# A second loop of pairs behind one branch, early reads for the first loop, and 86 unread products in the attention

## Chip, cores and metric

One NeuronCore of a Trainium2 chip runs the whole kernel. The metric is the device time of one execution in microseconds (us); three timed executions of the kernel before are known, and one more was taken with the hardware profiler. The engines are TensorE (PE; PEld is its weight load), VectorE (DVE), ScalarE (ACT), GpSimd (POOL) and SyncE (SP), which issues most DMAs. A q behind an engine's name means its sequencer.

## The reference

A Nyström attention with 32 landmarks over 8 batches, 8 heads, 576 tokens and 64 dimensions is followed by two mixture-of-experts layers on 4608 tokens with 8 experts each, top 1. Which expert gets how many tokens is known only at run time.

```python
A = sm(q, k_lm); Bm = sm(q_lm, k_lm); C = sm(q_lm, k)
Z = Bm.transpose(0, 1, 3, 2) / (norm(Bm, 1) * norm(Bm, inf) + 1e-06)
for _ in range(6):
    Z = 2 * Z - Z @ Bm @ Z
x = (A @ Z @ C @ v)            # rows of 512
for e in range(E):             # layer 0
    h = np.maximum(x[mask] @ w1[e], 0.0)
    out[mask] = gate_w[mask, None] * eom[mask, e, None] * (h @ w2[e])
for e in range(E):             # layer 1, routed by x @ w_gate + modality_bias
    h = np.maximum(x[mask] @ w1[e], 0.0)
    out[mask] = gate_w[mask, None] * (h @ w2[e])
```

## The kernel before

**Attention.** The work of the 8 batches is cut into small steps. A string `ORDER` lists them, a word each (batch and step), and the generators of the steps are advanced in that order, so it sets the order of the instructions on every engine. Its last words are `0st` and `0tab`: `st` is `static`, the first four tiles of layer 0's MoE (128 tokens each, the busiest expert's first 512 rows), and `tab` is `tile_table`, which works out on DVE, from the experts' counts, a table with one partition per further tile: the row to load, the piece of weights to load, and the parity (`PAR`). `numi` holds the number of tiles and of experts at work. Rows of tokens are scattered by POOL into a DRAM region `reg` with one stretch per expert (`scatter`, L684 clears a few words, L685 is the indirect DMA); `k.scat` lists these DMAs.

**A tile.** `steps` runs `h = relu(x @ w1)` (L1271) and `y = h @ w2` (L1322). Values are split into a high and a low fp16 part (`whi`, `wlo`; `hh` from ACT at L1279, `hl` from DVE at L1282), with three products for each. `xl` holds the 1024 x 128 transposed tokens, loaded by a DMA transpose from SP (L1066); `PLANS` says behind which product each other part runs (`after1`: the next tile's `xl`, behind the last product that reads this one). `L1152` is the product of the routing of the tile before, `L1143` the copy into the rows of the next layer, `L1203` their scatter.

**Loops.** Behind the static tiles eight products (L1692) are issued whose result nobody reads. Then every engine reads two registers (`reg_load`, L836, from `pari` and `numi`), SP loads the first rows (`x_load` in `tiles`), and `tiles(0, ...)` loops over the remaining tiles of layer 0, 34 with these inputs. Three static tiles of layer 1 follow, and then `tiles(1, ...)`, whose turns take two 128-row tiles at once (`pair`, products of 256 columns, L1388 and L1415, tokens in `xab`) or a single one (`alone`). With these inputs all its 17 turns are pairs. Each turn picks one of four bodies by two branches:

```python
with tc.If(odd > 0) as c:
    with tc.If(par < 2) as d:
        alone_(1)
    with d.Else():
        pair_(1)
```

TensorE, and every other engine, runs its instructions in the order in which they are written, and register reads and branches stand in that order too.

Of the kernel before, what the change touches and what calls it, by code (L numbers as in the profile page):

```python
# [26 lines left out]
E = 8  # L27
# [31 lines left out]
1mb0 1w0 2sc0 2sa0 1w1 1ws 3t2 2sc0 2sc1 1mb1 3t0 0x0 1ws 1ws 0x0 1mb0 3t3 2sc1 1ws 2sa0 2sa0 2ct0 2sc1 1mb1 1ws 2n
1ws 2n 1ws 2sa0 1ws 0x0 0f1 2ct0 2n 0f1 2ct1 2sa1 2ct1 0f1 1wg1 2sa1 3ld2 1wk0 2bt0 0f1 2ct1 2ct1 2sa1 2cv1 2n 1wk1  # L60
1wg1 2sa1 0f1 1wg1 2n 3t3 1wg0 2ct0 0x0 2bt1 0f1 3t2 2cv1 1wg1 2ma0 1wg0 2ma1 0f1 3t5 2n 3ld3 1wg0 1wg0 0x0 2ct0
0f1 2ma0 4ld2 1x3 3t0 2n 0f1 1x3 1x3 3t4 2bt0 2n 4ld0 0f1 1x1 2bt1 1x1 1x3 1x1 3t5 0f1 1x3 3t6 2cv0 3t6 2ma0 2ma1
1x1 2n 3sc0 2cv0 1x1 0f1 2ma1 4t5 3t4 2bt0 0f1 2bt1 0f1 1x4 1x4 0f1 1x4 2ch0.0 3sc0 0f1 3sc0 3t7 2ch0.1 2ch0.1
2ch1.1 2ch0.0 4t1 2ch1.0 1x4 2mb1 3sc0 2ch1.1 2ch1.0 0f1 1x2 1x4 2mb0 2mb1 2mb0 2mb0 2ch2.1 1x2 2ch2.0 1x0 4t0
2ch2.1 2ch2.0 1x2 2mb1 2ch3.1 2ch3.0 2ch3.1 2ch3.0 1x2 3t7 2ch4.1 1x2 2ch4.1 2ch4.0 3ct0 4t5 1x0 2ch4.0 4t0 0f2
2mb0 3ct0 2ch5.1 2mb0 2mb1 1x0 2ch5.0 2ch5.0 3sc1 0s1 2w0 2w0 1f1 3ct0 2ch5.1 2mb1 0s2 2w1 3ct0 4t4 2w1 3sc1 1f1
3sc1 2ws 3sa1 3sc1 1f1 0s3 2ws 3sa1 3sa0 3sa0 3n 3n 3sa0 3ct1 3sa0 3n 4t4 3ct1 2ws 2ws 3n 3ld4 3ct1 0s0 2ws 3sa1 3n
2ws 3ct1 0s4 2ws 3cv0 2ws 2wk0 2wg1 1f1 3sa1 1x0 3cv0 1f1 2wg0 3ma1 3bt0 4ld3 3n 2wg1 2wg1 2wg0 3n 1f1 4ld1 3n 2wk1
2wg1 1x0 1f1 3bt1 3cv1 2wg0 3ma1 4t1 4t2 4t3 3n 2wg0 3ma1 3cv1 3bt0 3bt1 2x1 3ma0 3bt1 4t6 2x2 4t7 2x1 2x1 3bt0
3ch0.1 3mb1 3ch0.1 3ch0.0 2x1 4t2 2x2 3ch1.1 1f1 3ch0.0 2x2 1f1 2x2 3ch1.1 5ld0 2x1 3ch2.1 1f1 4t3 3ch1.0 1f1 2x2  # L70
1f1 5ld2 1f1 1f1 3mb1 2x3 4sc0 1f1 3mb1 3ch1.0 2x3 3ma0 5t4 3ch2.0 3ch2.1 4t6 2x3 4t7 1f1 2x3 3ch2.0 3ch3.1 2x3
4sc0 3ch3.1 3ch3.0 3ch3.0 4sc0 0c 4sc1 3ch4.1 4sc1 1f1 3ch4.0 4sc1 3ma0 4sc0 4ct0 3ch4.0 3ch4.1 3ch5.0 4ld4 3ch5.1
4sc1 3mb0 3ch5.0 2x0 3ch5.1 4n 3mb0 2x4 4n 4ct0 5t0 1f2 3w1 3mb1 1s2 3w0 4sa1 5t4 3mb0 3mb1 4n 1s4 3mb0 3w1 3w0 3ws
2x4 4n 1s1 4sa1 3mb0 4ct1 4bt0 3ws 4sa1 4n 2x4 4ct1 3ws 4sa1 2x0 1s3 5ld3 2x4 3ws 4sa0 2x0 4n 4ct1 4ma1 2f1 4sa0 4n
2x0 4sa0 4ma1 3ws 4ct1 2x4 4n 3ws 4n 5ld1 4cv1 4bt0 1s0 3ws 4sa0 3ws 4bt1 6ld3 2x0 4bt0 4cv1 4ct0 3wg1 3wk1 4bt1
2f1 3wg1 4ct0 2f1 4cv0 3wg1 4ma1 3wg0 4bt1 4cv0 4ma0 2f1 3wg1 4ch0.1 3wg0 5t0 4ch0.1 4ch0.0 2f1 3wg0 4ch0.0 3wk0
2f1 4ch1.1 4mb1 3wg0 4ma0 4ch1.0 2f1 4ch1.1 4ma0 5t2 3x3 4ch1.0 3x3 3x3 3x1 3x1 5t3 4mb1 4ch2.1 4ch2.0 3x3 4mb0 2f1
6ld2 2f1 6t7 4ch2.1 4ch2.0 3x1 3x3 4ch3.0 4mb0 5t2 5t6 3x1 4ch3.1 5t1 3x0 2f1 5t3 4mb1 4ch3.0 4ch4.0 2f1 3x1 4ch3.1
2f1 3x0 2f1 5t6 3x0 4ch4.0 6t7 3x2 5ld4 4ch4.1 5t5 4ch4.1 3x0 4mb1 3x0 5t7 4mb0 2f1 5t1 4ch5.0 2f1 4ch5.1 4ch5.1
4ch5.0 5sa0 3x4 3x2 3x2 3x4 2f1 4w1 4w0 4mb0 5t5 3x4 4mb1 3x2 5t7 4mb0 5sa1 5sa0 3x2 2f1 6t5 5sa1 3x4 3x4 4w1 5sc1  # L80
3f1 4w0 2f2 5sc0 4ws 5sc1 2s0 4ws 5sa1 2s3 3f1 5sc1 6t6 5sc0 5sc0 5sa0 5sa1 4ws 3f1 5sa0 5sc1 5sc0 3f1 4ws 2s1 2s4
3f1 5ct1 5n 4ws 7ld2 5n 3f1 5ma0 5ct1 5ct1 3f1 5ct1 4ws 5ct0 5ct0 5n 5ct0 5ct0 5cv1 3f1 3f1 4ws 6ld0 5cv1 3f1 4ws
4wg0 3f1 3f1 5bt0 4wg0 2s2 5n 7t4 5cv0 3f1 3f1 6t6 4wk1 5n 6t5 4wg1 4wk0 4wg0 5cv0 5n 5bt1 4wg1 7ld3 5n 5ma0 4wg0
5n 4wg1 5bt0 4wg1 5bt1 5n 4x4 4x2 6t4 5bt0 5bt1 5ch0.0 5ma1 5ma0 7t5 3f1 4x4 5ch0.1 4x4 4x2 5ch0.0 4x4 0late 5ch0.1
5ch1.1 6t4 6ld1 5ch1.0 4x4 6sc1 7t4 3f1 5ch1.1 5ch2.1 5mb0 0late 6t1 5ch1.0 5ma1 6sc1 4x2 4x2 5ch2.0 3f1 5ma1 6t2
6sc1 5ch2.1 4x2 4x3 5ch2.0 5mb1 5ch3.1 7t5 6sc1 5ch3.0 0late 5ch3.1 4x3 4x1 5ch3.0 6t2 5mb1 3f2 5ch4.1 6t1 4x3
5ch4.0 0late 4x1 5mb0 5ch4.0 3s4 5ch4.1 7t6 4x3 6t3 4x1 5mb1 6ct1 5ch5.0 3s2 6t3 5ch5.0 6t0 5ch5.1 7t7 4x1 4x3 6ct1
5ch5.1 0late 5w0 5mb0 6t0 5w0 5w1 7t7 5w1 5ws 6sc0 4x1 7t6 4x0 5ws 5ws 6ld4 0late 6sc0 6sc0 5mb1 3s3 6sa1 5ws 5mb1
3s1 6sc0 6ct1 5ws 6sa1 6n 6sa1 5ws 6n 5mb0 6ct1 7ld1 4x0 5mb0 6n 6ct0 6sa0 5ws 6sa1 6cv1 6n 6ct0 5ws 6bt1 3s0 7ld0
6sa0 4x0 5wg1 6n 6bt0 6sa0 4f1 0late 5wg0 4f1 5wk1 6cv1 5wg1 5wk0 7t2 5wg1 6n 6sa0 4x0 5wg0 5wg0 5wg1 4f1 6n 4f1  # L90
4f1 5wg0 6bt1 6bt0 4x0 0late 6ct0 6n 4f1 6ct0 5x1 4f1 6cv0 5x1 6n 0late 6bt1 5x1 6ch0.1 5x4 7t0 5x1 6cv0 6bt0 6ma1
5x1 7t1 5x4 5x4 6ch0.0 6ma0 4f1 7sc1 4f1 7t3 7ld4 5x4 6ma1 6ch0.1 4f1 7t3 4f1 4f1 6ma0 6ch1.1 7t0 6ch0.0 6ma1 4f1
7sc1 5x4 7sc1 6ch1.0 6ch1.1 6ch1.0 5x2 7t1 6ch2.0 6mb1 4f1 7sc1 0late 7t2 6ch2.1 4f1 6ch2.1 7sc0 0late 5x2 6ch3.1
5x2 6ch2.0 6ma0 5x2 4f1 4f1 7sc0 5x2 7sc0 6ch3.0 4f2 6ch3.0 7ct1 6ch3.1 6ch4.0 0late 6ch4.1 7sc0 6ch4.1 7n 0late
# [218 lines left out]
def attention(tc, k, ctx, qk, v, pairs, singles, consts, late, third, static, table):  # L313
# [388 lines left out]
    def begin(b, name, *args):  # L702
# [6 lines left out]
        if name == "tab":  # L709
            return table()  # L710
        if name == "st":
            pairs.pop(), singles.pop()
            return static(bank)
# [24 lines left out]
ET = mybir.EngineType  # L738


PAR, CUT, PUT, LOAD, PIECE_NO, ROW, LAST, PART, PAIR, NF = range(10)
HALF = DM // 2


# [1091 lines left out]
```

## Time and profile before

| What | Value |
| --- | --- |
| median of 3 executions | 1032.93 us (1027.84 to 1040.15) |
| profiled execution, its own time | 1032.47 us |
| its span, first to last instruction | 1030.8 us |
| mean granted TensorE clock | 0.968 |
| TensorE busy | 958.1 us (93%) |
| VectorE, ScalarE, GpSimd busy | 714.6, 426.1, 229.5 us |
| TensorE busy from 300 to 650 us | 348.60 us |

In time: the attention fills the first 217 us, the static tiles of layer 0 run from 195 to 258 us, the first loop from 261 to 649, the static tiles of layer 1 to 670.7, the second loop from 681 to 1016. Idle times are given in brackets behind an instruction, with the engine that ended them; "issue" means that the profile shows nothing that was waited for. [...]

### The profile page before, as it was taken

What the parts mean: (1) busy time and instruction counts of PE and PEld (TensorE: products, weight loads), DVE (VectorE), ACT (ScalarE), POOL (GpSimd) and SP (SyncE); (2) the same over time, 40 slices, a digit from 0 to 9 for tenths busy, and PEclk for the clock granted to TensorE, in tenths of its full rate; (3) what the DMA queues carried; (4) which work ended last, traced back from release to release, by engine and by line L of the source; (5) the groups of instructions that cost most, each with busy time, mean ns of one, the idle gap of its engine ahead of it and who ended that gap; (6) DMA issues with size and microseconds to landing.
All of it is one profiled execution on the core that took longest, in us unless ns stands there. A gap on an engine that the chain in (4) does not pass through costs nothing. (4 is left out here: it accounts for less than half of the span.)

```text
span 1030.8 us, 35844 instructions
## 1 busy us (share of the span) xinstructions
PE 958.1 (93%) x11491; PEld 730.6 (71%) x11492; DVE 714.6 (69%) x2714; ACT 426.1 (41%) x994; POOL 229.5 (22%) x341
## 2 busy tenths in 40 slices
PE   6888879989799999999999999969999999999995
PEld 3554545656677777767777677648888888888885
DVE  6788978848477877778777777925467676546543
ACT  3575657732243433433434333323344444334332
POOL 6566776535010010100100001100100110110010
PEclk9998989989899999999999999989999999999998
DMA  8656665629366472365663346332212112121220
GB/s 276 189 187 233 221 245 178 196 80 295 85 158 159 129 179 59 73 164 144 159 154 70 83 111 185 89 69 51 61 42 62 42 52 69 45 62 42 61 62 31
DMA packets 164470, 125.08 MB, mean 121 GB/s; under 512 B 135710, under 2 KB 135710, under 8 KB 163376
## 3 DMA queue, kind: packets, MB, share of 16 engines
q1 hardware_dynamic: 153664, 95.16, 34.7%
q0 software_dynamic: 9008, 28.95, 7.5%
q8 instruction: 42, 0.69, 0.3%
q10 hardware_dynamic: 1728, 0.06, 0.1%
q14 instruction: 28, 0.23, 0.1%
HBM read 60.48 MB, written 34.57 MB: 92 GB/s over the span
## 5 line engine op out<-in xcount | busy, mean ns | idle before, releaser
L1271 PE MATMUL b_hp<-xl,whi 128*128 128x128 f16 x2368 | 208.4, 221 | 1.8 <-DMA xl<-reg 1.8
L1271 PE MATMUL b_hp<-xl,wlo 128*128 128x128 f16 x1184 | 206.0, 221 | 0.0
L1271 PEld LDWEIGHTS <-whi 128*128 128x128 f16 x2624 | 202.2, 99 | 5.1 <-issue 4.1
L1388 PE MATMUL b_hp<-xab,whi 128*128 128x256 f16 x1088 | 181.1, 274 | 10.3 <-issue 10.3
L1388 PE MATMUL b_hp<-xab,wlo 128*128 128x256 f16 x544 | 149.2, 274 | 0.4 <-DVE tf L821 0.4
L1271 PEld LDWEIGHTS <-wlo 128*128 128x128 f16 x1312 | 129.8, 99 | 0.0
L1322 PE MATMUL ybank<-wlo,hh 128*128 128x512 f16 x328 | 124.8, 381 | 0.1
L1322 PE MATMUL ybank<-whi,hh 128*128 128x512 f16 x328 | 124.8, 380 | 0.0
L1388 PEld LDWEIGHTS <-whi 128*128 128x128 f16 x1088 | 106.4, 98 | 25.0 <-issue 12.2
L1322 PE MATMUL ybank<-whi,hl 128*128 128x512 f16 x328 | 122.6, 381 | 0.0
L1203 POOL DMA_INDIRECT reg<-rows,si x38 | 37.8, 994 | 360.4 <-DVE rr L1134 314.8
L1126 ACT ACTIVATE rt<-ybank,sc 128x512 f16<-128x512 f32 x38 | 26.1, 687 | 208.6 <-DVE off L1584 195.3
L807 DVE SCALAR_TENSOR_TENSOR wlo<-stg,whi x76 | 92.8, 1221 | 25.5 <-ACT whi L802 20.3
L1322 PEld LDWEIGHTS <-hh 128*128 128x128 f16 x656 | 62.4, 98 | 66.7 <-issue 1.0
L1224 POOL DMA_INDIRECT out_dram<-osbb,tokb x17 | 16.7, 983 | 268.1 <-ACT osbb L1240 268.1
L1344 DVE SCALAR_TENSOR_TENSOR s<-b_hp,r 128x256 f32<-128x256 f32 x34 | 14.4, 423 | 88.1 <-ACT r L1343 85.9
L802 ACT ACTIVATE whi<-stg x38 | 72.5, 1907 | 0.0
L1279 ACT ACTIVATE hh<-b_hp 128x512 f16<-128x512 f32 x74 | 44.2, 597 | 52.8 <-PE b_hp L1271 30.3
L1110 DVE TENSOR_REDUCE sc<-ybank 128x1 f32<-128x512 f32 x38 | 26.2, 691 | 53.2 <-PE L1271 42.7
L1322 PEld LDWEIGHTS <-hl 128*128 128x128 f16 x328 | 32.2, 98 | 39.9 <-issue 1.0
L1388 PEld LDWEIGHTS <-wlo 128*128 128x128 f16 x544 | 53.5, 98 | 7.6 <-DVE tf L821 0.6
L1415 PEld LDWEIGHTS <-sh 128*128 128x128 f16 x544 | 53.1, 98 | 7.0 <-ACT sh L1353 0.9
(443 smaller groups left out, 2120.4 us busy)
## 6 DMA issues: line engine op xcount, KB each, us to landing
stg<-in_wall_dram SPq DMA_DIRECT2D x29, 1024.0 KB, 5.5
kq<-in_qk_dram SPq DMA_DIRECT2D x32, 576.0 KB, 5.4
v<-in_v_dram SPq DMA_DIRECT2D x8, 1024.0 KB, 9.8
reg<-zrow SPq DMA_DIRECT2D x18, 264.0 KB, 7.6
v<-in_v_dram SPq DMA_DIRECT2D x8, 128.0 KB, 9.7
s<-in_wall_dram SPq DMA_DIRECT2D x1, 1024.0 KB, 5.4
xl<-reg SPq DMA_TRANSPOSE x42, 3.3
mt<-reg SPq DMA_DIRECT2D x41, 8.0 KB, 4.3
```

Source lines behind the costliest of these rows:

```text
L802: return self.tc.nc.scalar.activation(self.slot(self.ws[d].hi, i), self.slot(self.stg, i), AF.Copy, scale=WS)
L807: return self.tc.nc.vector.scalar_tensor_tensor(self.slot(w.lo, i, a), self.slot(self.stg, i, a), WS, self.slot(w.hi, i, a), op0=ALU.mult, ...
L1110: v.tensor_reduce(sc[:, 0:1], y, axis=AX.X, op=ALU.max, apply_absolute_value=True)
L1126: a.activation(rt[:, 0:DM], y, AF.Copy, scale=sc[:, 1:2])
L1203: w = nc.gpsimd.indirect_dma_start(out=k.reg[:, :], out_offset=bass.IndirectOffsetOnAxis(ap=self.si.bitcast(U32), axis=0), in_=rows, in_of ...
L1224: return nc.gpsimd.indirect_dma_start(out=self.out[:, :], out_offset=bass.IndirectOffsetOnAxis(ap=tok.bitcast(U32), axis=0), in_=osb, in_o ...
L1271: mm = nc.tensor.matmul(hp[ft // 4][:, ft % 4], lhsT=ww[c][:, ft * P:(ft + 1) * P], rhs=self.xl[:, x], start=n == 0, stop=n == 11)
L1279: self.read[i] = [nc.scalar.activation(hh[:, 4 * i:4 * i + 4], hp[i], AF.Relu)]
L1322: nc.tensor.matmul(self.y, lhsT=a[:, ft], rhs=ww[ft], start=n == 0, stop=n == 23)
L1344: v.scalar_tensor_tensor(s[:, 2, c], h[:, :, 0], 0.0, r21[:, c], op0=ALU.max, op1=ALU.subtract)
L1388: nc.tensor.matmul(hp[ft // 2][:, ft % 2], lhsT=ww[c][:, ft * P:(ft + 1) * P], rhs=self.xab[:, x], start=n == 0, stop=n == 11)
L1415: nc.tensor.matmul(bank[:, half[0]], lhsT=l[:, c], rhs=r[c], start=new and c == 0 and i == 0, stop=c == 3 and i == 2, skip_group_check=not ...
```

## The change

It does four things. (1) `ORDER` gets ten words `0fillN`: together 86 products of a 128 x 128 identity with itself into the next bank of the pool, never read. (2) The clearing of words in the scattered rows moves from each scatter (five per batch) to one memset per batch. (3) In layer 0's table, `pari` is worked out right behind `numi`, and both registers are read there by all engines; the row of the first loop's first tile is worked out early in a tile of its own (`rowi`); and the fourth static tile's `after1` issues that load (`x_next`), which before stood at the loop's entry. The eight unread products stay. (4) The second loop knows pairs only: the table counts tiles of 256 rows and has a second row field `ROWB`; tokens and their words come with two DMAs each in place of one; one branch on the parity picks the body. Two clears ahead of the loops go.

```diff
+    def fill(n):
+        while True:
+            idle = singles[(turn[1] + 1) % len(singles)][:, 0:P]
+            for _ in range(n):
+                nc.tensor.matmul(idle, lhsT=k.ident16, rhs=k.ident16, start=True, stop=True)
+            yield
...
+        nc.gpsimd.memset(mi32[:, :, 2:8], 0)
...
     def scatter(st, t):
-        nc.gpsimd.memset(st.rows[0:m, t, DM + 2:DM + 8], 0)
...
     v.tensor_copy(numi, num)
     yield
+    if not pairs:
+        _, _, rowi, pari, parf = out
+        v.tensor_single_scalar(pari, numi[:, 1:2], 1, op=ALU.bitwise_and)
+        v.tensor_copy(parf, pari)
+        yield
+        k.second, k.nt = reg_load(tc, pari[0:1, 0:1], 1), reg_load(tc, numi[0:1, 0:1], P - 1)
+        yield
...
     def m_load(self, reg, row):
-        if self.second == "pair":
-            return self.tc.nc.sync.dma_start(out=self.mab, in_=reg[ds(row, 2 * P), DM:ROWI].rearrange("(a p) m -> p a m", a=2))
+        if self.second:
+            for n in range(2):
+                self.tc.nc.sync.dma_start(out=self.mab[:, n], in_=reg[ds(row[n], P), DM:ROWI])
+            return
...
-        def x_load(kind, row):
-            with tc.If(kind > 1) as c:
-                self.x_load(reg, nc.s_assert_within(row, 0, row_max - P, skip_runtime_bounds_check_because=WHY), self.xab)
-            with c.Else():
-                self.x_load(reg, row)
+        def x_load(rows):
+            for n, row in enumerate(rows):
+                self.x_load(reg, row, self.xab[:, :, n * P:(n + 1) * P])
...
-            first = self.x_load(reg, row0)
-            after(tc, [d for _, d in k.scat] + k.fill, first)
-        nt = reg_load(tc, numi[0:1, 0:1], P - 1)
+        nt = reg_load(tc, numi[0:1, 0:1], P - 1) if layer else k.nt
...
             if layer:
-                odd = nc.s_assert_within(par & 1, 0, 1, skip_runtime_bounds_check_because=WHY)
-                with tc.If(odd > 0) as c:
-                    with tc.If(par < 2) as d:
-                        alone_(1)
-                    with d.Else():
-                        pair_(1)
+                with tc.If(par > 0) as c:
+                    self.pair(wts.ws[1], load, after1, spots(1))
                 with c.Else():
-                    with tc.If(par > 1) as d:
-                        pair_(0)
-                    with d.Else():
-                        alone_(0)
+                    self.pair(wts.ws[0], load, after1, spots(0))
...
+        def x_next():
+            r = moe.x_load(k.reg, reg_load(tc, rowi[0:1, 0:1], 2 * E * CAP - P, (ET.SP,)))
+            after(tc, [d for _, d in k.scat] + k.fill, r)
+            apart(tc, k.scat2, r)
...
-    second = reg_load(tc, pari[0:1, 0:1], 1)
+    second = k.second
```

Where the instructions stand now. On TensorE, in batch 0 of the attention, the first fill comes ahead of the product with the weights `w` (L609, in the new file L608). Before:

```order
L577 MATMUL bank_113<-dg_736,ones 128x128
L505 MATMUL bank_114<-ident,cx_0_573 128x128 x4
L346 MATMUL bank_115<-bt_0_678 32x32 x4
L346 MATMUL ybank<-bt_1_638 32x32 x4
L609 MATMUL bank_113<-ident,w_690 64x128
L511 MATMUL bank_114<-ident,cx_0_573 64x128
```

After, with the last of the 14 products:

```order
L703 LDWEIGHTS ident_63
L703 MATMUL bank_113<-ident_63 128x128
L608 MATMUL bank_113<-ident,w_693 64x128
L510 MATMUL bank_114<-ident,cx_0_576 64x128
L608 MATMUL bank_115<-ident,w_693 64x128
```

The products stand directly ahead of L609's and write the bank that it writes next.

On TensorE the two register reads stood behind the eight unread products (L1692), at the first loop's entry. Before:

```order
L1692 LDWEIGHTS ident_63
L1692 MATMUL pair_110<-whi_118,ident_63 128x128
L836 TENSOR_LOAD pari
L836 TENSOR_LOAD numi
L1448 COMPARE_AND_BRANCH
L1448 UNCONDITIONAL_BRANCH
```

After, they are among the third static tile's first products (L1280 is L1271 of before):

```order
L1280 MATMUL pair_111<-xl,wlo_119 128x128
L1280 LDWEIGHTS whi_118
L845 TENSOR_LOAD pari
L845 TENSOR_LOAD numi
L1280 MATMUL pair_111<-xl,whi_118 128x128
```

They moved up by a tile and a half; 36 products of that tile's first layer, its second layer and the whole fourth tile now stand behind them.

On DVE, the steps of the table between the fourth static tile's two low parts `hl` (L1282, in the new file L1291). Before, from the second `hl` on:

```order
L1282 SCALAR_TENSOR_TENSOR hl<-pair_111,hh 128x512
L994 SCALAR_TENSOR_TENSOR tab_tab<-tab_q 128x1
L997 TENSOR_SCALAR tab_tab<-tab_q 128x1
L999 SCALAR_TENSOR_TENSOR tab_tab<-tab_q,tab_tab 128x1
L1000 TENSOR_TENSOR tab_tab<-tab_q 128x1
L1002 COPY tab_tab<-tab_sums 128x1
L1006 CAST tabi<-tab_tab 128x9
L1143 COPY rows<-rt 128x512
```

After, up to the second `hl`:

```order
L1014 CAST tab_tab<-rowi 128x1
L1015 TENSOR_SCALAR tab_tab<-tab_q 128x1
L1017 SCALAR_TENSOR_TENSOR tab_tab<-tab_q,tab_tab 128x1
L1018 TENSOR_TENSOR tab_tab<-tab_q 128x1
L1020 COPY tab_tab<-tab_sums 128x1
L1024 CAST tabi<-tab_tab 128x10
L1026 TENSOR_SCALAR tabi<-tabi 128x1
L1027 TENSOR_SCALAR tabi<-tabi 128x1
L1028 TENSOR_TENSOR tabi<-tabi 128x1
L1291 SCALAR_TENSOR_TENSOR hl<-pair_111,hh 128x512
L1161 COPY rows<-rt 128x512
```

The end of the table, which stood behind the second `hl`, stands ahead of it now: 37 instructions between the two `hl` in place of 17, and three in place of ten between `rt` (L1130) and the counts ahead of the first. On SP the two reads stand between the transfer of `yt` and that of the fourth tile's `xl`, and the first loop's first `xl` follows that tile's other transfers.

## Rows read from the trace of the kernel before

**Rows 1.** Windows view: window, busy us (count) of PE, PEld, DVE, ACT, POOL; clock; DMA.
```profile
700.00:1000.00 300.00, 298.90 (x2726) 265.49 (x2725) 177.98 (x472) 118.98 (x277) 29.78 (x31) 1.00 0.20 53
```

**Rows 2.** Timeline at the second loop's entry (start, us), and the tile view of xab.
```profile
666.67 2.13 SPq L1066 DMA_TRANSPOSE xab<-reg  x1
...
680.98 0.59 PE L1388 MATMUL b_hp<-xab,whi 128*128 128x256 f16 x2 [10.28 <-issue]
...
DMA to landing us min/median/max: 6.6/6.6/6.6
```

**Rows 3.** Timeline of PE, third static tile to the first loop's second turn.
```profile
237.16 0.22 PE L1271 MATMUL pair<-xl,whi 128*128 128x128 f16 x1
...
246.91 0.27 PE L1271 MATMUL pair<-xl,whi 128*128 128x128 f16 x2 [2.15 <-DMA xl<-reg]
...
255.43 0.38 PE L1322 MATMUL ybank<-whi,hl 128*128 128x512 f16 x1
...
257.59 0.61 PE L1692 MATMUL pair<-whi,ident 128*128 128x128 f16 x8
260.89 0.34 PE L1152 MATMUL b_lp<-g2s,yt 128*128 128x16 f16 x8 [2.69 <-SPq L1448]
263.01 0.37 PE L1271 MATMUL b_hp<-xl,whi 128*128 128x128 f16 x2 [1.78 <-DMA xl<-reg]
...
278.53 0.34 PE L1152 MATMUL b_lp<-g2s,yt 128*128 128x16 f16 x8 [2.00 <-issue]
```

**Rows 4.** Windows view of PE alone: window, busy us (count), clock, DMA share, GB/s.
```profile
40.30:43.60 3.30, 2.07 (x79) 1.00 0.35 135
43.60:47.00 3.40, 3.40 (x52) 0.50 0.72 198
...
210.90:217.70 6.80, 4.49 (x16) 0.50 0.03 12
...
263.00:268.90 5.90, 5.89 (x58) 0.50 0.46 128
...
675.20:685.30 10.10, 4.32 (x21) 0.50 0.38 129
```

**Rows 5.** Source view of L1537, whole run and 670 to 682; DMA view 668 to 681.
```profile
L1537 PEldq COMPARE_BRANCH  x8: 215/215/6067, 674.7 to 820.1; - x8
...
L1537 PEldq COMPARE_BRANCH  x1: 6067/6067/6067, 674.7 to 674.7; - x1
...
q8 instruction: 3, 0.05, 2.0%
```

**Rows 6.** Timeline of a turn of the second loop; DMA share by fortieths, 693 to 703.
```profile
693.90 2.14 SPq L1066 DMA_TRANSPOSE xab<-reg  x1
...
702.75 0.38 PE L1388 MATMUL b_hp<-xab,whi 128*128 128x256 f16 x2
...
DMA  0000000006799999970000000000005100000000
```

**Rows 7.** Source view of L836 (register reads), 255 to 264: ns min/median/max.
```profile
L836 PEldq TENSOR_LOAD <-pari x1: 483/483/483, 257.7 to 257.7; - x1
...
L836 PEldq TENSOR_LOAD <-numi x1: 310/310/310, 258.3 to 258.3; - x1
```

**Rows 8.** Timeline of DVE during the third and fourth static tiles.
```profile
240.49 0.15 DVE L930 CAST numi<-tab_num 128x2 int32<-128x2 f32 x1
...
252.69 0.14 DVE L1104 TENSOR_SCALAR ok<-mt 128x1 f32<-128x1 int32 x1
...
254.53 0.67 DVE L1282 SCALAR_TENSOR_TENSOR hl<-pair,hh 128x512 f16<-128x512 f32 x1
```

**Rows 9.** Timeline of SP: the load of the fourth static tile's tokens.
```profile
239.61 3.19 SPq L1066 DMA_TRANSPOSE xl<-reg  x1
```

**Rows 10.** Timeline of PE at the places of the first and last fills.
```profile
41.48 0.30 PE L609 MATMUL bank<-ident,w 128*64 128x128 f32 x1 [2.05 <-DVE w L589]
...
213.14 0.61 PE L633 MATMUL pair<-wb,at 64*128 64x144 f32 x2 [4.19 <-DVE third_i L1645]
```

More of the change, by code (lines that the diff above doesn't have):

```diff
@@ L111 @@
+0tab 0tab 0st 0st 0st 0st 0st 0st 0st 0st 0st
 """
@@ L738 @@
 ET = mybir.EngineType
-PAR, CUT, PUT, LOAD, PIECE_NO, ROW, LAST, PART, PAIR, NF = range(10)
+PAR, CUT, PUT, LOAD, PIECE_NO, ROW, LAST, PART, PAIR, ROWB, NF = range(11)
 HALF = DM // 2
@@ L880, in t @@
         return sp.tile(shape, dt, name=f"tab_{name}", tag=f"tab_{name}")
-    tabi, numi = out
+    tabi, numi = out[0:2]
     c, act, key, n, m = (t(x, [P, E]) for x in ("c", "act", "key", "n", "m"))
     ni, cmp, wide = t("ni", [P, E], I32), t("cmp", [P, E, E]), t("wide", [P, E, E])
-    val, sums, num, nx, x2 = t("val", [P, 6, E]), t("sums", [P, 6]), t("num", [P, 2]), t("nx", [P, 2]), t("x2", [P, 2])
+    val, sums, num, nx, x2 = t("val", [P, 5, E]), t("sums", [P, 5]), t("num", [P, 2]), t("nx", [P, 2]), t("x2", [P, 2])
     tab, q = t("tab", [P, NF]), t("q", [P, 11])
-    at, left, runs, isa, isb, e, pc, x, l2, ta, tl = (q[:, i:i + 1] for i in range(11))
+    at, left, runs, isa, isb, e, pc, x, l2, ta, xb = (q[:, i:i + 1] for i in range(11))
     pos = val[:, 2]
-    s0, sn, sp_, send, spre, st = (sums[:, i:i + 1] for i in range(6))
+    s0, sn, sp_, send, spre = (sums[:, i:i + 1] for i in range(5))
+    size = 2 * P if pairs else P
     v.memset(tab[:, PART:NF], 0.0)
@@ L908, in tile_table @@
     v.scalar_tensor_tensor(n, ni, 4.0, act, op0=ALU.max, op1=ALU.mult)
-    if pairs:
-        half, two = t("half", [P, E], I32), t("two", [P, E])
-        v.tensor_copy(val[:, 5], n)
-        v.tensor_single_scalar(half, ni, 1, op=ALU.arith_shift_right)
-        v.tensor_scalar(two, n, -4.0, 0.0, op0=ALU.add, op1=ALU.max)
-        v.tensor_tensor(two, two, half, op=ALU.min)
-        v.tensor_sub(n, n, two)
     v.reduce_sum(num[:, 1:2], act, axis=AX.X)
@@ L937, in tile_table @@
     yield
-    rows = 6 if pairs else 5
-    v.tensor_tensor(val[:, 0:rows], val[:, 0:rows], m.unsqueeze(1).to_broadcast([P, rows, E]), op=ALU.mult)
+    v.tensor_tensor(val, val, m.unsqueeze(1).to_broadcast([P, 5, E]), op=ALU.mult)
     yield
-    v.reduce_sum(sums[:, 0:rows], val[:, 0:rows], axis=AX.X)
+    v.reduce_sum(sums, val, axis=AX.X)
     yield
     v.tensor_sub(at, k.tidx, s0)
+    if not pairs:
+        v.tensor_sub(left, sn, at)
+        yield
+        v.scalar_tensor_tensor(l2, left, -float(P), send, op0=ALU.mult, op1=ALU.add)
+        yield
+        v.tensor_tensor(l2, l2, spre, op=ALU.max)
+        yield
+        v.scalar_tensor_tensor(rowi, left, 0.5, l2, op0=ALU.is_ge, op1=ALU.mult)
+        yield
     for i in range(2):
@@ L982, in tile_table @@
     v.tensor_mul(e, nx[:, 0:1], isa)
-    v.scalar_tensor_tensor(x, tl, -float(P), send, op0=ALU.mult, op1=ALU.add)
+    if pairs:
+        v.scalar_tensor_tensor(x, left, -float(size), send, op0=ALU.mult, op1=ALU.add)
+        v.scalar_tensor_tensor(xb, x, float(P), spre, op0=ALU.add, op1=ALU.max)
     yield
@@ L986, in tile_table @@
     v.scalar_tensor_tensor(e, nx[:, 1:2], isb, e, op0=ALU.mult, op1=ALU.add)
-    v.tensor_tensor(x, x, spre, op=ALU.max)
+    if pairs:
+        v.tensor_tensor(x, x, spre, op=ALU.max)
     yield
@@ L1425, in tiles @@
         tc, nc, k, wts = self.tc, self.tc.nc, self.k, self.wts
-        reg, self.loop, self.second = k.reg, True, "alone" if layer else False
+        reg, self.loop, self.second = k.reg, True, bool(layer)
         row_max = 2 * E * CAP - P
@@ L1449, in tiles @@
             i = nc.s_assert_within(i, 0, P - 2, skip_runtime_bounds_check_because=WHY)
-            par = field(i, PAR, 7 if layer else 1)
-            row = field(i, ROW, row_max, (ET.SP,))
+            par = field(i, PAR, 1)
+            row = [field(i, f, row_max, (ET.SP,)) for f in (ROW, ROWB)] if layer else field(i, ROW, row_max, (ET.SP,))
             if layer:
@@ L1608, in run @@
     tab, num = pool.tile([P, NF], I32, name="tabi"), pool.tile([P, 2], I32, name="numi")
+    rowi, pari = (pool.tile([P, 1], I32, name=x) for x in ("rowi", "pari"))
+    par = pool.tile([P, 1], F32, name="par")
     def late():
@@ L1681, in static @@
             yield from moe.steps(wts.ws[0], ("first", "second", "route", "route")[s], lambda: m_load(s),
-                                 (lambda: x_load(s + 1)) if s < 3 else None, between=done if s == 3 else None)
+                                 (lambda: x_load(s + 1)) if s < 3 else x_next, between=done if s == 3 else None)
     def table():
-        yield from tile_table(tc, k, pool, k.cnt[0], k.first[0], start[0], None, moe, (tab, num), False)
+        yield from tile_table(tc, k, pool, k.cnt[0], k.first[0], start[0], None, moe, (tab, num, rowi, pari, par), False)
     k.unread = pairs[0][:, 0, 0:P]
```

197 lines of the change are left out of this document (84 added, 113 removed), and 1 row of the table PLANS.

## The prediction

> **What bounds the kernel now.** I read the windows of 50 us first, and in them the share of TensorE. Inside both loops it never stops for long: 298.90 of 300 us in the second [rows 1], the first is alike in the table above. Nothing that another engine does faster there can shorten the span; only fewer products could, and the counts of these inputs give the second loop pairs alone already in the kernel before (its 17 tiles all run the arm with 256 columns), so its products stay. What can be won lies outside: at the two loop entries, and in the attention, where TensorE pauses. The waits of TensorE and its timeline come next. At the entry of the second loop it does nothing for 10.28 us [rows 2]; at the entry of the first for 2.69 and 1.78 us, and ahead of the fourth static tile for 2.15 [rows 3]. [...]
>
> **The second loop's entry.** The 10.28 us are not a wait for data. The first rows' transfer is issued at 666.67 and takes 6.6 us to land, so at 673.3 [rows 2]; yet the first product is at 680.98. The source view of the inner branch, L1537, shows why: TensorE's sequencer (PEldq) spends 6.067 us on it from 674.7 on, against a median of 0.215 over its eight executions [rows 5], and the DMA view of these microseconds has three transfers of instructions on queue 8 [rows 5]. In the kernel before, the tile's parity picks an arm and a second branch jumps over the whole unpaired body to the paired one. That jump is in the first turn, which is odd (only odd turns execute L1537, eight of 17, and the first start is 674.7). In the changed kernel an odd tile falls from its one branch straight into the paired body. The jump is gone, and with it up to 6.07 - 0.2 = 5.87 us. What is late next is the second of two transfers: the 256 rows now come as two DMAs, and SP was busy 2.13 us with issuing the one [rows 2], so the second lands about 2 us behind the first, near 675.3, against 674.9 for the branch. I take the transfer: first product at 675.3, **-5.7 us**. If the code behind the remaining branch has to be fetched too, the gain is 0. The clock: from 675.2 to 685.3 it is 0.50, and TensorE worked 4.32 us of that [rows 4], which costs 2.2. With 4.6 us of idleness instead of 10.3 the stretch may go or may move under more work (5.89 us in the stretch at the first loop's entry, 2.9 lost); taken as unchanged, bounds -2.2 to +0.8.
>
> [...]
>
> **The second loop's turns.** Each turn issues two transposes in place of one, and two small loads for the rows' words. The transpose of the next pair is issued at 693.90, and its packets pass in one burst (the DMA share by fortieths of the ten microseconds from 693: slices 10 to 18, so up to 697.5); the products that read it begin at 702.75 [rows 6]. A second issue of about 2.1 us fits in those 5 us: cost 0. On DVE, ACT and POOL nothing of a turn changes. Bounds: -1 to +1 us for all 17.
>
> **The first loop's entry and what is paid for it.** The reads of two registers (pari, numi) stand behind the eight unread products in the kernel before, take 0.483 and 0.310 us on TensorE [rows 7], and the first rows' transfer, L1066, follows on SP; TensorE waits 2.69 us for SP and 1.78 for the rows [rows 3]. The change issues that transfer behind the last product that reads the fourth tile's xl, so it lands beside that tile's y products, and reads the registers earlier. The 1.78 go, and of the 2.69 the jump into the loop may stay: the nearest row is the loop's own next turn, where TensorE starts after 2.00 us of "issue" (L1152 at 278.53) [rows 3]. So 4.47 becomes 2.0 at the cautious end and about 0 at the other; I take 2.0, **-2.5**.
>
> The payment is new waits. The reads now stand on all five engines behind numi's CAST in the table's order, and on TensorE that place is among the third static tile's first products: by counting its products it is where the row at 237.16 stands [rows 3]. numi is written at 240.49 for 0.15 [rows 8], pari by one more instruction of 0.07, the two reads take 0.79: TensorE goes on at about 241.5, **4.4 us idle**. Queued behind: the rest of that tile's products and its y. The 2.15 us that TensorE waited ahead of the fourth tile take up a part, but that wait moves as well: SP issued the fourth tile's xl at 239.61 [rows 9], now it first waits for pari and issues at about 241.5, 1.9 later. So the fourth tile starts max(4.4 - 2.15, 1.9) = 2.2 us later. If the order of the table's steps lets DVE reach numi sooner, it is 0. Second, DVE: the fourth tile's second hl stood 17 instructions behind the first (1.84 us from 252.69 to 254.53, 0.108 each) [rows 8], and now 37 stand between; ahead of the first hl seven fewer. That is 20 x 0.108 - 7 x 0.108 = 1.4 us later against the tile's start; hl was there at 255.2 (254.53 and 0.67) and its first reader is at 255.43 [rows 3, 8]: 1.4 - 0.2 = **+1.2**. On POOL the reads stand between scatters, and the single memset per batch takes one memset and its wait out of each scatter but the first; no TensorE instruction of these stretches waits for a scatter: 0.
>
> The clock at the first loop: 263.0 to 268.9 at 0.50 with 5.89 us of work costs 2.9 [rows 4]. With the entry shorter it may not fall; but the 4.4 us pause at 237 may bring a fall there (3.4 us, as the shortest stretch in rows 4, so 1.7 lost). I take half of the 2.9, **-1.5**. Together: +2.2 + 1.2 - 2.5 - 1.5 = **-0.6**, between -7.4 (nothing paid, the whole entry and its clock won) and +2.6 (2.2 + 1.2 + 1.7 - 2.5).
>
> **The 86 products.** [...] They stand ahead of instructions that waited anyway: 14 ahead of L609 (2.05 us), 22 ahead of L633 (4.19) [rows 10], which need 1.1 and 1.7; the eight other sites are shorter waits with four to ten products. Cost 0, bound +2 if some of these waits have moved. The gain could only be the clock: 43.6 to 47.0 is at 0.50 with 3.40 us of work (1.7 lost), 210.9 to 217.7 with 4.49 (2.2) [rows 4]. The 14 products come before the first of these; the 22 come at 213, when the clock is already down, and can only end that stretch earlier. I take the first, **-1.7**, bounds 0 and -3.9.
>
> [...]
>
> **Sum.** -5.7 - 0.6 - 1.7 = -8.0 from the profiled execution's 1032.47, which lies 0.46 below the median: **1024.5 us**. About 1%, 10.3 us, is what a measurement of this kernel tells from no change (its three runs spread over 1.2%).
>
> **Rivals.** (a) *Everything adds*: DVE reaches numi before TensorE asks, the first loop starts with its rows there, the clock stays up at one entry and in two stretches of the attention: -5.7 - 6 - 3.8 = 1017. For it: all the parts exist in rows. Against: the place of the reads. Chance 0.22. (b) *The stall stays*: the fetch at the second loop's entry comes at another instruction, since the loop's head is itself reached by a jump. Then 1032.5 - 0.6 - 1.7 = 1030. Against it: the branch that took 6.07 us lies behind that head, and what follows it in the changed kernel is the next row of code. Chance 0.13. (c) *Slower*: the second transpose of each pair. It decides if the two together with the two small loads take over 8.8 us from issue to landing (702.75 - 693.90) where one took 3.6 (to 697.5); each microsecond beyond is paid in 16 turns, so 1 us gives 1040, 1.3 us 1045. Chance 0.06. (d) *The first loop's entry turns into a loss by the full +2.6*, with no gain in the attention: 1032.5 - 5.7 + 2.6 = 1029.5. Chance 0.09. The forecast, 1020 to 1029, has 0.50.
>
> **How the numbers follow.** Under 1022.6: (a) and a third of the forecast, 0.39. Over 1043: the worse half of (c) and what I have not seen, 0.05. Between: 0.56. The range leaves out the best of (a) and all of (c): 1013 to 1032.
>
> **What would show it.** In the profile after: TensorE's gap at the second loop's entry about 4.6 us, ended by a DMA; L1522, the new branch, at 0.2 us on its sequencer; a new wait of about 4 us in the third static tile's products, released by DVE; "L1152 <- SPq" of 2.69 and the xl wait of 1.78 gone; the stretch of low clock from 43.6 gone; TensorE in the second loop still at 298.9 of 300 us. I am wrong if the entry still shows 10 us, or pairs wait for xab.

## The result, and the profile after

The changed kernel takes 1023.8 us (median of 6, 1020.07 to 1028.2), the kernel before 1034.62 (median of 6, 1027.84 to 1040.15): ratio 0.989, 95% interval 0.985 to 0.994. In a later series (f1 below) it was 1021.59 against 1034.75, ratio 0.986 (0.982 to 0.991). Medians here and below are over all executions; two of the twelve of e4 and one of the kernel before beside e5 to e7 ran in a slower state, and the ratios leave these three out. The profiled execution of the changed kernel took 1025.7 us, with a span of 1024.0 and a mean clock of 0.971, above the median of its kind by 1.9; that of before took 1032.47, 2.2 below. The forecast was 1024.5.

The lines of the changed kernel that answer to those of before follow in time. First the places in the attention and at the loop entries [rows 4, 10] in the windows view (window, its length, busy us and count of PE, clock, DMA share, GB/s):

```profile
40.30:43.60 3.30, 2.28 (x84) 1.00 0.29 115
43.60:47.00 3.40, 2.91 (x70) 1.00 0.66 234
87.10:97.20 10.10, 9.38 (x118) 0.50 0.86 305
216.80:223.50 6.70, 6.42 (x32) 0.50 0.01 2
244.20:250.80 6.60, 4.00 (x37) 0.50 0.81 248
268.00:275.00 7.00, 6.94 (x117) 1.00 0.57 165
675.30:685.00 9.70, 9.66 (x89) 1.00 0.46 140
```

The clock is the one granted to TensorE, as a share of full speed. At 0.50 the products of 512 columns start every 0.43 us (L1322 in the kernel before: 216.10, 216.53, 216.95), at 1.00 every 0.22 (204.99, 205.21, 205.43), so half of the work at 0.50 is lost, which is how the prediction prices it. The low clock that stood at 43.6, at the first loop's entry and at the second's, each time in or behind idle time (of the 3.30 us ahead of 43.6 TensorE worked 2.07 [rows 4]; for the entries [rows 2, 3]), is gone; the attention still has stretches of it (one is the row from 87.1), as have the static tiles at 216.8, and the third static tile has a new one at 244.2. TensorE's timeline from that tile to the second pair (start, us, what, idle before):

```profile
238.54 0.27 PE L1280 MATMUL pair<-xl,whi 128*128 128x128 f16 x2
...
246.80 0.37 PE L1280 MATMUL pair<-xl,whi 128*128 128x128 f16 x2 [4.70 <-issue]
...
256.13 0.27 PE L1280 MATMUL pair<-xl,whi 128*128 128x128 f16 x2
...
266.66 0.39 PE L1331 MATMUL ybank<-whi,hl 128*128 128x512 f16 x1 [1.94 <-DVE hl L1291]
...
268.83 0.61 PE L1680 MATMUL pair<-whi,ident 128*128 128x128 f16 x8
269.49 0.34 PE L1170 MATMUL b_lp<-g2s,yt 128*128 128x16 f16 x8
269.72 0.27 PE L1280 MATMUL b_hp<-xl,whi 128*128 128x128 f16 x2
...
291.12 0.35 PE L1170 MATMUL b_lp<-g2s,yt 128*128 128x16 f16 x8
...
641.43 0.22 PE L1280 MATMUL b_hp<-xl,wlo 128*128 128x128 f16 x1 [1.49 <-issue]
...
653.19 0.27 PE L1280 MATMUL b_hp<-xl,whi 128*128 128x128 f16 x2 [1.61 <-issue]
...
675.34 0.38 PE L1397 MATMUL b_hp<-xab,whi 128*128 128x256 f16 x2 [1.58 <-DMA xab<-reg]
...
695.34 0.38 PE L1397 MATMUL b_hp<-xab,whi 128*128 128x256 f16 x2 [0.19 <-issue]
```

Against [rows 3]: a new pause of 4.70 us in the third static tile, no wait ahead of the fourth (256.13), a new 1.94 us for its second hl, and then an entry into the first loop with no pause at all (268.83, 269.49, 269.72), where 2.69, 1.78 and, a turn later, 2.00 us stood. Two pauses that the kernel before did not have stand in the static tiles of layer 1, at 641 and 653. Against [rows 2] the entry of the second loop is 1.58 us in place of 10.28.

The pause of 4.70 ends in "issue", since the profile counts register reads as no work. DVE's timeline and the source view of the reads (ns min/median/max, first and last start) name it:

```profile
245.27 0.16 DVE L932 CAST numi<-tab_num 128x2 int32<-128x2 f32 x1
245.47 0.15 DVE L936 TENSOR_SCALAR pari<-numi 128x1 int32<-128x1 int32 x1
```

```profile
L845 PEldq TENSOR_LOAD <-pari x1: 636/636/636, 245.7 to 245.7; - x1
...
L845 PEldq TENSOR_LOAD <-numi x1: 379/379/379, 246.4 to 246.4; - x1
```

pari is there at 245.62 (245.47 and 0.15), TensorE's two reads run from 245.7 to 246.8, and the product behind them starts at 246.80.

At the second loop's entry, the source view of the one branch, and SP's timeline with the tile view of xab:

```profile
L1522 PEldq COMPARE_BRANCH  x25: 71/194/700, 672.6 to 991.5; - x25
```

```profile
669.33 2.65 SPq L1082 DMA_TRANSPOSE xab<-reg  x2
...
L1082 SPq DMA_TRANSPOSE xab<-reg x36: 1231/1254/1300, 669.3 to 1004.6; - x36
```

The branch's median is 0.194 us and its longest 0.700, where L1537 had one of 6.067 [rows 5]. Two transposes of 128 rows take 1.25 us each to issue, not 2.1, and both are there 6 us after the first is issued (675.34 less 669.33). The windows view of the second loop:

```profile
700.00:1000.00 300.00, 298.44 (x2730) 266.54 (x2729) 178.76 (x475) 119.04 (x280) 29.55 (x30) 1.00 0.21 53
```

Its turns run as before [rows 1]. To compare places in time, the start of the same product is taken in both profiles. Two that are needed stand here for the kernel before, the third static tile's first product and the third turn of the first loop:

```profile
233.76 0.27 PE L1271 MATMUL pair<-xl,whi 128*128 128x128 f16 x2
...
290.98 0.35 PE L1152 MATMUL b_lp<-g2s,yt 128*128 128x16 f16 x8
```

The changed kernel stands at the third static tile's start +4.8 us (238.54 against 233.76), at the fourth's +9.2 (256.13, 246.91), at the first loop's third turn +0.1 (291.12, 290.98), at the end of layer 1's static tiles +3.1 (the second loop's first product less the pause ahead of it, 673.76 and 670.70), at the second pair -7.4 (695.34, 702.75), and at the end of the span -6.8.

### The profile page after: what moved, and what is told of

Read it like the earlier page. It is cut to its first block, busy times and chain, and to the rows that moved or that the text cites. A ratio compares the mean times of both kernels' runs of the same rounds, so it can differ in the third digit from the quotient of the medians.

```text
span 1024.0 us, 36104 instructions
## 1 busy us (share of the span) xinstructions
PE 962.2 (94%) x11577; PEld 733.9 (72%) x11578; DVE 710.0 (69%) x2708; ACT 426.5 (42%) x993; POOL 227.1 (22%) x308
## 5 line engine op out<-in xcount | busy, mean ns | idle before, releaser
L1280 PEld LDWEIGHTS <-whi 128*128 128x128 f16 x2624 | 200.6, 98 | 9.2 <-issue 8.2
L1280 PE MATMUL b_hp<-xl,whi 128*128 128x128 f16 x2368 | 204.3, 219 | 1.6 <-issue 1.6
L1280 PE MATMUL b_hp<-xl,wlo 128*128 128x128 f16 x1184 | 202.0, 219 | 1.5 <-issue 1.5
L1280 PEld LDWEIGHTS <-wlo 128*128 128x128 f16 x1312 | 129.0, 98 | 0.0
## 6 DMA issues: line engine op xcount, KB each, us to landing
stg<-in_wall_dram SPq DMA_DIRECT2D x29, 1024.0 KB, 5.6
v<-in_v_dram SPq DMA_DIRECT2D x8, 1024.0 KB, 6.2
s<-in_wall_dram SPq DMA_DIRECT2D x1, 1024.0 KB, 5.5
```

Of the source, the lines that this page charges most:

```text
L1280: mm = nc.tensor.matmul(hp[ft // 4][:, ft % 4], lhsT=ww[c][:, ft * P:(ft + 1) * P], rhs=self.xl[:, x], start=n == 0, stop=n == 11)
```

## The experiments

All times are medians, with the ratio to the kernel before on the same chip. The kernels tried are called e1 to e7 and f1 to f4, in the order in which they stand. In the first series (before: 1034.56) four kernels ran.

**Without the fills (e1).**

```diff
-... 0fill14 ... 0fill4 ... 0fill22 ...
```

> The changed kernel without its 86 unread products; the rest of the change stays. Theory A (the fills lie inside waits and keep the clock up): they cost nothing and save about one stretch of low clock, so without them the attention is 1 to 2 us longer and the kernel stands at 1025 to 1026 us, ratio to the kernel before about 0.991. Rival B (the fills do nothing that lasts: the profiled execution of the changed kernel lost 4 us in the attention against that of before, with 13 stretches of low clock against 11): without them the time is the same or up to 2 us shorter, 1022 to 1024, ratio 0.987 to 0.990. Since the code on TensorE gets shorter by 172 instructions, a third reading is tested on the side: the two new pauses of 1.49 and 1.61 us at 641 and 653 us, which end in issue, come from where the code's blocks end and move or vanish here; if they come from the static tiles' own work they stay.

1031.12 us, 0.997 (0.994 to 1.000): 7 us slower than the changed kernel was, though on another chip. That is far more than either theory gave. The pauses bear out the third reading: those at 641 and 653 are gone, and others are there. Its waits of TensorE are nearly those of the same kernel run again later (f3, shown below).

**Late reads (e2).**

```diff
-        k.second, k.nt = reg_load(tc, pari[0:1, 0:1], 1), reg_load(tc, numi[0:1, 0:1], P - 1)
...
+    k.second, k.nt = reg_load(tc, pari[0:1, 0:1], 1), reg_load(tc, num[0:1, 0:1], P - 1)
     second = k.second
```

> The changed kernel with the reads of pari and numi put back behind the eight unread products, ahead of the first loop; the early load of the first rows stays. Theory A (the early reads stop TensorE in the third static tile, 4.70 us in the changed kernel's profile, and pull the clock down there): the pause is gone, the static tiles end 4 to 6 us earlier, the entry pays 1 to 2 us for the reads, and the kernel is 2 to 5 us faster than the changed one: about 1020 us, ratio to before 0.985 to 0.987. Rival B (what the reads cost is only moved to the entry, where all five engines wait for each other again): 1023 to 1025, ratio 0.989 to 0.991, with a new wait of some 3 us ahead of the loop's first product.

1020.05 us, 0.987 (0.983 to 0.991). The waits of TensorE from 225 to 275 (us in total, times, longest), here and then in the changed kernel:

```profile
PE ybank L1330 <- DVE hl L1290: 2.4, 1, 2.4
PE bank L1169 <- DMA yt<-rt: 2.0, 1, 2.0
PE pair L1279 <- DMA xl<-reg: 0.6, 1, 0.6
PE bank L1207 <- DVE mx L1197: 0.4, 1, 0.4
...
```

```profile
PE pair L1280 <- issue: 4.7, 1, 4.7
PE ybank L1331 <- DVE hl L1291: 1.9, 1, 1.9
...
```

The 4.7 us are gone, and at the entry nothing came back; but the fourth tile now waits 2.0 and 0.6 us for transfers that the pause had covered, the counts (L1207) 0.4 for DVE, and hl is later by 0.5. So of the 4.7 us 1.2 are left, and the trace agrees: from the third static tile's first product to the loop's third turn it takes 51.3 us (234.96 to 286.27), the changed kernel 52.6. The clock falls here too, only later (0.51 from 260.8 to 264.2). In time the ratio lies between the changed kernel's own two (0.989 and 0.986), so this kernel can't be told from it.

**Fills alone, in the kernel before (e3).**

```diff
...
+        if name == "fill":
+            return fill(*args)
...
+... 0fill14 ... 0fill4 ... 0fill22 ...
```

> The kernel before with the ten fill words in its order and nothing else. Theory A: 1 to 2 us faster than before, ratio 0.998, the low clock from 43.6 to 47 us gone. Rival B: no difference that lasts, ratio 0.999 to 1.001, the stretches of low clock fall at other places but not less often. Rival C: the products come late and push what stands behind them, 86 times 0.056 to 0.11 us in all: 3 to 8 us slower, ratio 1.003 to 1.008.

1035.78 us, 1.002 (1.000 to 1.005): no gain. But the entry of the second loop, which no line of this kernel changes, is no longer 10.28 us, and pauses in "issue" stand elsewhere (waits of TensorE, 275 to 900):

```profile
PE b_hp L1397 <- issue: 8.2, 3, 4.6
PE b_hp L1280 <- issue: 3.5, 2, 1.8
```

The entry takes 4.6 of the 8.2 us, a later pair 3.0, and layer 1's static tiles 3.5 in two pauses, as in the changed kernel; the second turn's 2.00 us [rows 3] are gone. Nothing but the 172 instructions of the fills on TensorE was added. So where such pauses stand depends on what is added ahead, and the two at 641 and 653 come with these instructions; whether it is their number or their work, the later runs tell.

**The second loop alone, in the kernel before (e4)** (part 4 of the change; order, table of layer 0, scatters and the first loop's entry as before).

> The kernel before with the second loop alone changed (pairs only, one branch, two transposes and two small loads per pair, table of 256-row tiles); order, fills, early reads and first load as before. Theory A (the entry's 10.28 us were a fetch behind the inner branch): the entry shrinks by 6 to 9 us, the clock there gives up to 2 more, the turns stay: 8 to 10 us faster than before, ratio 0.990 to 0.992, so this part alone holds all of the measured gain. Rival B (the entry's gain needs the early start of the rest or the pauses of 1.5 us each in the static tiles of layer 1 come with this part): 4 to 6 us faster, ratio 0.994 to 0.996.

1032.79 us, 0.998 (0.996 to 1.001). Theory A fails in its size: the 10.28 us did shrink, to 3.0, but the second pair got a pause of 3.3 (waits, 275 to 900):

```profile
PE b_hp L1377 <- issue: 3.3, 1, 3.3
PE b_hp L1377 <- ACT osb L1230: 3.0, 1, 3.0
```

The 3.0 stand at the entry, the 3.3 at the second pair. From the end of layer 1's static tiles to the second pair the profile gains 4.2 us (27.8 in place of 32.1), where the changed kernel gains 10.5. So this part alone does not hold the gain.

The second series, on a chip on which the kernel before took 1041.38, was to test the code's position.

**Fills moved to one early place, narrow (e5).**

```diff
-... 0fill14 ... 0fill4 ... 0fill22 ...
...
     for _ in range(WARM):
         nc.tensor.matmul(k.unread, lhsT=ident16, rhs=ident16, start=True, stop=True)
+    for _ in range(86):
+        nc.tensor.matmul(k.unread[:, 0:16], lhsT=ident16, rhs=ident16[:, 0:16], start=True, stop=True)
```

> The changed kernel with its 86 unread products taken out of their ten places and 86 narrow ones (16 columns in place of 128) put behind the 82 unread products that both kernels issue early in the attention. All code behind the last of the ten places stands at the same position as in the changed kernel; the fills no longer stand in the waits. Theory A (the 7 us that the changed kernel loses without fills come from where the blocks of its code end: 172 instructions of TensorE more or less): the time is that of the changed kernel, 1021 to 1026 us, ratio 0.987 to 0.991, the pause at the first loop's second turn (2.60 us without fills) is absent and so is that of 3.1 us at the second pair. Rival B (they come from the clock that the fills hold up in the attention): the time is that without fills, 1029 to 1033, ratio 0.995 to 0.998.

1035.13 us, 0.9945 (0.991 to 0.998): a ratio between those of the two theories, with no pause at the second turn or the second pair. Its profiled execution, 1028.55, is one of the two fastest of twelve.

**All fills, and 64 narrow products more (e6)** (the same three lines with 64).

> The changed kernel with 64 narrow unread products (16 columns) more at the same early place: its code on TensorE behind it stands 128 instructions further on, and everything else is the same. They take about 2 us of TensorE's time at most where it also waits. Theory A (block ends): pauses that end in issue appear or vanish at the first loop's second turn, the static tiles of layer 1 and the second loop's first two pairs, and the time moves by 3 to 8 us, most likely up: 1027 to 1032, ratio 0.993 to 0.998. Rival B (clock): no such pause changes, 1022 to 1027.

1034.89 us, 0.994 (0.991 to 0.997), inside theory A's range by its ratio (the chip is slower than the one that the times were given for), with a pause of 2.7 us at the first loop's second turn and of 3.0 at the second pair (waits, 275 to 900):

```profile
PE b_hp L1399 <- issue: 3.0, 1, 3.0
PE b_lp L1172 <- issue: 2.7, 1, 2.7
```

That profile is of its slowest execution, 1043.36.

**Late reads, and the table's end behind hl (e7).** The late reads of above, and in the order's tail one `0st` ahead of the last ten `0tab`.

```diff
-... 0tab 0tab 0tab 0tab 0tab 0tab 0tab 0tab 0tab 0tab 0st ...
+... 0st 0tab 0tab 0tab 0tab 0tab 0tab 0tab 0tab 0tab 0tab ...
```

> The changed kernel with the two register reads at the first loop's entry (as in the run with late reads) and with the last ten table steps behind the step of the fourth static tile that issues its second hl, in place of ahead of it. Theory A (the 1.9 to 2.4 us that TensorE waited for hl in the changed kernel and in the run with late reads are the table's steps ahead of it on DVE): that wait is gone, 1 to 2.4 us faster than the run with late reads, 1018 us, ratio 0.984 to 0.986. Rival B (the table is then late for the loop's first reads of it): the wait moves to the loop's entry, 1020 to 1022, ratio 0.986 to 0.989.

1027.62 us, 0.988 (0.983 to 0.993). The wait for hl is gone, and rival B's ratio came: another wait of 1.78 us, for DVE, stands in the first turn of the loop (timeline). It is for mx, a step of the routing, and not for a read of the table, so of rival B's reason only that DVE is behind is shown; and this profile has 3.8 us ahead of the fourth tile's tokens, which the others do not have.

```profile
272.89 0.17 PE L1207 MATMUL b_rk<-oh,tri 128*128 128x8 f16 x1 [1.78 <-DVE mx L1197]
```

The third series set the two readings of the fills against each other, four kernels on one chip (before: 1034.75).

The expectations of f1 to f4, in this order:

> The changed kernel itself once more, as the measure for the three beside it on the same chip. It is the case with the fills in their waits and the code where the change puts it. Expected by every theory: ratio to before near 0.989, and pauses of TensorE ending in issue only in the static tiles of layer 1 (about 1.5 us each).

> The changed kernel with 42 narrow unread products (84 instructions, about 1 us) more early in the attention. [...] Theory A (code position decides): pauses of 2.6 us at the first loop's second turn and of 3 us at the second loop's first two pairs come back, and the time is 5 to 8 us over f1. Rival B (the fills' clock decides): the time of f1 within 2 us, no such pauses.

> The changed kernel without fills, again beside f1. Theory A: 5 to 8 us over f1, like f2. Rival B: the same 5 to 8 us, but f2 stays at f1.

> The changed kernel without fills in the waits and with 86 narrow products early in the attention, so its code behind stands as in f1. Theory A: the time of f1, up to 2 us more for the narrow products. Rival B: the time of f3. If it lies half way, both count.

The edits are those above (f2 is the early narrow products with 42 beside all fills; f3 and f4 are the kernels of e1 and e5 again). In f2 the code stands 84 instructions further on than in the change, and so 256 from its place in f3.

| | code as in the change | code as without fills, or 256 further |
| --- | --- | --- |
| fills in the waits | f1: 1021.59, 0.986 (0.982 to 0.991), clock 0.979 | f2: 1026.77, 0.992 (0.989 to 0.995), clock 0.978 |
| no fills in the waits | f4: 1028.49, 0.994 (0.991 to 0.997), clock 0.972 | f3: 1030.67, 0.996 (0.993 to 0.998), clock 0.968 |

The clock is the mean over all executions of a kernel (6, 10, 12 and 12). Waits of TensorE from 275 to 900, f2 and then f3, f1 and then f4:

```profile
PE b_hp L1399 <- issue: 2.9, 1, 2.9
PE b_hp L1399 <- PEq L847: 2.5, 1, 2.5
PE b_lp L1172 <- PEq L1815: 2.4, 1, 2.4
```

```profile
PE b_hp L1396 <- issue: 3.1, 1, 3.1
PE b_lp L1169 <- issue: 3.0, 1, 3.0
PE b_hp L1396 <- PEq L844: 2.8, 1, 2.8
```

```profile
PE b_hp L1280 <- issue: 3.3, 2, 2.2
PE b_hp L1397 <- DMA xab<-reg: 1.4, 1, 1.4
```

```profile
PE b_hp L1281 <- issue: 3.2, 2, 1.9
...
PE b_hp L1398 <- DMA xab<-reg: 1.3, 1, 1.3
```

The pauses go with the column, not with the row: f1 and f4 have the same, f2 and f3 have the second loop's 2.5 to 3.1 twice (f2 has the third at another place than f3, ahead of layer 1's static tiles, not at the loop's second turn). The second pair's pause has a name: it is one execution of the loop's branch on TensorE's sequencer. The source view of that branch from 690 to 697 (ns min/median/max), f1 and then f3:

```profile
L1522 PEldq COMPARE_BRANCH  x2: 71/194/316, 691.3 to 692.8; - x2
```

```profile
L1521 PEldq COMPARE_BRANCH  x2: 81/1871/3661, 690.9 to 695.8; - x2
```

The longest execution of this branch is 3.51 us in f2, 3.81 in e4 and 3.52 in e6, which have the pause too, and 0.58 in f4. Behind the pauses the clock falls as well (0.57 from 694 to 698 in f2, 0.69 from 695.0 to 700.5 in f3).

The times need both. As measured, the column is worth 5.2 us with fills and 2.2 without (this one is not clear of noise: -1.4 to 5.0 by resampling the executions), the row 6.9 and 3.9. But f2 and f4 also pay for their narrow products. Timeline of f4, then f2, the narrow ones and the product behind them:

```profile
25.09 2.30 PE L185 MATMUL pair<-ident 128*128 128x16 f16 x86
27.24 0.28 PE L511 MATMUL bank<-ident,cx 128*64 128x128 f32 x1
```

```profile
24.90 1.10 PE L186 MATMUL pair<-ident 128*128 128x16 f16 x38
...
26.49 0.28 PE L512 MATMUL bank<-ident,cx 128*64 128x128 f32 x1
```

They hold up what follows by 2.15 and 1.59 us. If that is paid in full at the end, which is an estimate, the column is worth 3.6 and 4.4 us and the row 4.7 and 5.5, and the four times agree: about 4 us for the place of the code, about 5 for the fills. The row's part shows in the clock, 0.979 and 0.978 against 0.972 and 0.968. So both theories are right in part. Where in the attention the fills gain is not shown: the profiled executions of f1 and f4 took the same time (1023.71 and 1023.61) at the same clock (0.978), f4's being the fastest of its twelve. What is left of the gain without the fills and at the other place of the code is f3 against the kernel before, 4.1 us. Parts 2 and 3 of the change were not tried alone.

## Why the prediction came out

The time was right, within 1 us, and the parts were not. Against the profiled execution, the parts missed by -4.8, -4.0, +6.5 and +2.9 us, in the order below, and cancel; that the sum fits so well is luck.

*Second loop's entry, forecast -5.7.* The branch that took 6.07 us is gone, and the entry waits for the second transpose, at 675.34 where 675.3 was given. That the branch waited for instructions is my reading: the profile shows transfers of instructions beside it, three from 668 to 681 [rows 5] and one from 666 to 676 in the changed kernel, but names no wait for them. The size was not right: from layer 1's static tiles to the second pair the profile gains 10.5 us (+3.1 to -7.4). Two terms were mis-sized. "The clock, taken as unchanged" was 2.2 us of gain, at the bound I gave: with 1.58 us of idleness it does not fall (675.3 to 685.0 at 1.00). And "about 2 us behind the first" with 6.6 us to land made 4.6 us from the last y to the first product; the two smaller transposes were there 6 us after the first issue, not 8.7, which leaves 1.58. That the time of the first product came out as said, 675.34, is chance: all stood 3 us later by then. And the gain is not a property of the part: with the code placed otherwise it is 3 us at the entry and 3 at the second pair (e4, f3). Rival (b), a stall that comes back at another instruction, was true of e4, f2 and f3, where it comes back on the branch that is left, and untrue only at the place where the change puts the code. The longest execution of that branch is 3.51 to 3.81 us there, 0.700 in the changed kernel and 0.58 in f4; so that a jump as such brings the stall, the reason that rival (b) gives, is not shown.

*First loop, forecast -0.6.* The pause that I priced at 4.4 was 4.70, hl's 1.2 was 1.94. What failed is the fourth tile's 2.2: it was 4.4 (+4.8 to +9.2), since in the pause and behind it the clock was down from 244.2 to 250.8 (4.00 us of work at 0.50, so 2.0 lost), which I had priced as 1.7 in the bound but not in the sum. On the other side I kept 2.0 us of the entry and half of its clock; in truth everything went, 2.69, 1.78, 2.00 at the second turn, 2.9 of clock behind it [rows 3, 4] and 1.6 behind the second turn, 11 us, of which hl took 1.9. That last stretch is this row of the kernel before (windows, PE):

```profile
279.20:282.40 3.20, 3.20 (x34) 0.50 0.03 3
```

From the third tile's start to 291 us that is -4.6 in place of -0.6. The second turn's 2.00 did not go by the early reads but by the instructions added ahead: they are gone with the fills alone (e3) and are there as 2.6 to 3.0 us in the runs without fills and with 64 more products (e1, f3, e6).

*Fills, forecast -1.7.* The profiled execution stands 4.8 us later at the third static tile, so by it the fills would have cost. It is one execution: the runs of the third series, 40 in number, show a gain of about 5 us. The stretch from 43.6 went as said. The 1.1 and 1.7 us for 14 and 22 products are that many times 0.076, an eighth of the 0.61 that L1692's eight took [rows 3]; in the changed kernel the 22 took 1.39, from 212.75 (timeline), and the product behind them still waited 2.87 for DVE. The direction holds, and the size was taken too small. The trace of one execution could not have told it: six executions of one kernel run from 1019.59 to 1026.40 us, with clocks from 0.975 to 0.982 (f1).

*Not in the sum, +2.9.* The pauses of 1.49 and 1.61 us in layer 1's static tiles. Nothing in the diff touches these tiles; they are there in f4 without the fills and gone in f2 with them, so they go with the place of the code. I did not ask what 172 more instructions do to code that is not changed. That is the hole in the working: in these runs such pauses came or went with 84, 128 and 172 instructions more or less on TensorE (f2, e6, e1 and e3).

The second transpose costs nothing in the turns, as forecast (298.44 against 298.90 us of 300); rival (c) is out. From the second pair to the end the changed kernel loses 0.6 us (-7.4 to -6.8), inside the bound of 1. Reads that come late to all engines (e2) leave by the trace about 1 us more, which the times don't resolve.

## What to carry to other kernels

In this kernel the second pair's pause, which ended in "issue" just behind a jump, belonged to the place of the code and not to the work: the source view has it as one long execution of the branch (3.66 us in f3, where f1 has 0.32 at most in that stretch), and edits of 84 to 172 instructions ahead of it brought it or took it away. So look there first where code has loops and branches. An experiment that removes instructions should put as many back elsewhere, or it measures two things, and what the ones put back cost should be read from its trace. A pause cost its own length here and, where the clock fell with it, half of the work in that stretch more (4.70 us, and 2.0 of the 4.00 at 0.50); so shorten the pauses first and price the clock by the rows behind each of them. And when all engines read a register, put the read where its value is already there on all of them: what it stops is what is queued behind it, here 4.70 us of TensorE.

## What was not expected of the hardware

The position of the code moved the kernel by about 4 us of 1022 (f1 against f2; f4 against f3 agrees but is not clear of noise alone), and single pauses of 1.5 to 3 us came and went with it. 84 instructions more and 172 less, which differ by 256, have the same two pauses at the second loop (2.9 and 2.5 us in f2, 3.1 and 2.8 in f3), and a third at different places (2.4 and 3.0). That it takes 256 is not shown: 128 more than in the change, which is 44 more than in f2, had pauses too (2.7 and 3.0, e6). The profile shows instructions moved in transfers of about 16 KB (queue 8 of the kernel before: 42 with 0.69 MB in all); how many instructions one holds, and which of them an engine has at which jump, no run shows.

Unread products of 128 columns in waits of TensorE raised the mean clock of whole executions from 0.968 and 0.972 (f3, f4) to 0.978 and 0.979 (f2, f1). The kernel before did not gain from the same products (e3, clock 0.970 against 0.967 beside it). The pauses that they moved there took 3.5 us in layer 1 and 3.0 in the second loop, but gave 5.7 at its entry and 2.0 at the first loop's second turn. Its profiled execution is 3.2 us longer than that of before: it is 5.3 us later at the first loop's first tile (268.36 against 263.01), and behind the pause in the second loop the clock falls (0.52 from 863.6 to 867.1). But that is one execution; why there is no gain stays open.
